# A gated linear scan feeding a mixture of experts on one core: ScalarE's list in the second group, and the path of y and x through DRAM in groups three and four

## The chip, the core and the metric

The kernel runs on one core of one Trainium2 chip. The metric is the device time of one execution in microseconds (us). Engines are called TensorE (PE in the views: matmuls; PEld: its weight loads), VectorE (DVE), ScalarE (ACT), GpSimd (POOL) and SyncE (SP, which here does little but issue DMAs, in the order of its list).

## The reference, cut to what matters

```
# attention: B=4 batches, H=8 heads, S=768 steps, D=48; complex state S (D x D) per head
a = a * min(|a|, 0.999) / (|a| + 1e-6)          # complex gate, one per step and row d
for t in range(S):
    S = a[t][:, None] * S + k[t][:, None] * v[t][None, :]
    y[t] = q[t] @ S.real
x = y as [3072 tokens, 384]                      # heads side by side
# mixture of experts: E=4 experts, F=1024
p = probs / (probs.sum(-1) + 1e-9)
out = sum over e of p[:, e] * (relu(x @ w1[e]) @ w2[e])
```

## The kernel before, in words

The 3072 tokens are cut into 12 groups of 256 (three to a batch), numbered 0 to 11, and a group into two chunks of 128. The work falls into a first part, up to about 600 us of the profile, and a second.

In the first part the experts 0 and 1 are applied to one group after another by `moe1`. A group has eight pairs, numbered 0 to 7, of two 128-wide slices of F: `w1_step` makes `ph` (18 matmuls, L179), ScalarE makes `hh` (L188) and VectorE `hl` (L189) out of it, and `w2_step` (12 matmuls, L198) adds them into `po`, one pair later. Each product is made three times, of high and low parts: weights `whi`, `wlo`, activations `xha`, `xla`, and `hh`, `hl`. `ph3_2` is group 3's pair 2; `po` carries the number of the pair with which its expert began, so that `po3_0` gathers pairs 0 to 3.

While group g goes through `moe1`, the attention of group g+1 is made and the preparation of later groups goes on. For each group that is:

- `norm`: the gate is scaled. ScalarE and VectorE take turns on tiles `s`, `u` and `A`: squares (L322, L323), a sum (L324), Ln (L333), Exp (L334), Square (L342), a product (L343), Identity (L344), then L346, L348, L349 and the scaling of `A` (L351).
- `prefix`: cumulative products of `A` on VectorE (L359 to L362, L302 to L310).
- `finish` and `front`: ScalarE L421, L422, L427 and L428, VectorE L425, then `Q` (L430) and `K` (L445 to L449). From the third group on both go to DRAM and back (`q_d`, `k_d`, L459 and L466) into `Qst` and `Kst`, of which there is one each. Groups 0 and 1 turn K on TensorE instead (`ktp`, `kp`, with ScalarE evicting into `KT` and `Kst`).
- `attention`: `ktp` (K turned), `dp` (the state's increment, L518), `sc` (scores, L530), `yp` (values, L546 and L551), evicted into `y` by ScalarE (L558). Groups 0 to 2 turn y into x on TensorE (`xp`, L582). Later groups store y to DRAM (`store_y`, L623) and read it back as `xa` (`load_x`, L159); `split_x` makes `xha` (ScalarE, L166) and `xla` (VectorE, L168) of it, which the next group's `ph` reads.

`between(k)` is called ahead of pair k. At pairs `FIRST[g]`, +1 and +2 it takes the next piece of group g's attention; otherwise it advances the preparation by a budget of microseconds (`STEP`, `MORE`). A scheduler then decides the order of each engine's list by its own simulated times. `behind(a, b)` adds a dependency that only orders a after b on one engine, and so steers that scheduler. An engine works through its list in order, so that an instruction which waits holds up all that stand after it.

In the second part (`w1_full`, `w2_full`) experts 2 and 3 are applied to blocks of 512 tokens. The change touches nothing there.

Of the kernel before, what the change touches and what calls it, by code (L numbers as in the profile page):

```python
# [8 lines left out]
F32 = mybir.dt.float32  # L9
F32R = mybir.dt.float32r  # L10
AF = mybir.ActivationFunctionType
# [45 lines left out]
WARM = {6: "pq", 7: "tk"}  # L57
NSEL = 2
XSEL = 3
FIRST = {1: 5, 2: 5, 3: 4, 4: 4, 5: 3, 6: 3}  # L60
STEP = {1: 4.2, 2: 4.2, 3: 4.2, 4: 4.2, 5: 4.2}
MORE = (1.9, 1.9, 0.5)
HALF = (2, 3, 4, 5)
HOFF = 96
WIDE = 32 + P + 48
DMA_SCRATCH = 4096
# [2 lines left out]
def fast_path(ctx, tc, qkP, aP, vP, probsP, w, out, flag):  # L69
# [39 lines left out]
    def behind(ins, prev):  # L109
        tc.add_manual_dep(ins.ins, prev.ins.name,  # L110
                          mybir.DependencyInfo(mybir.DependencyClass.NoSync, mybir.DependencyReason.DATA),
                          reason="issue order")
# [41 lines left out]
        wts[i] = (hi, lo)  # L154
        return last_pe if ps is not None else None

    def load_x(g):
        x = moe.tile([P, NJ, G], F32, tag="x", name=f"xa{g}", bufs=1)
        nc.sync.dma_start(x, y_d[g].rearrange("(j p) t -> p j t", p=P))  # L159
        return [(slice(0, G), x)]  # L160

    def split_x(g, parts):
        xh = moe.tile([P, NJ, G], F32R, tag="xh", name=f"xha{g}")
# [65 lines left out]
    with ExitStack() as c1:  # L229
# [84 lines left out]
        def norm(g, A, parts=((0, SEG),), prev=(None, None)):  # L314
            s = tmp(f"s{g}")
            u = tmp(f"u{g}")
            for n, (lo, hi) in enumerate(parts):
                col = g if n == 0 else NG
                fs = slice(lo * MS, hi * MS)
                Af = A.rearrange("p c i m -> p c (i m)")[:, :, fs]  # L320
                m2, L, y0, v = s[:, 0, fs], s[:, 1, fs], u[:, 0, fs], u[:, 1, fs]
                ins = [nc.scalar.activation(m2, Af[:, 0], AF.Square)]  # L322
                sq = nc.scalar.activation(L, Af[:, 1], AF.Square)  # L323
                ins.append(nc.vector.tensor_tensor_reduce(m2, m2, L, scale=1.0, scalar=3e38,  # L324
                                                          op0=ALU.add, op1=ALU.min, accum_out=st_m2[:, col:col + 1]))
                for x, p in zip(ins + [sq], prev + prev[:1]):
                    if p is not None:
                        behind(x, p)
                if n > 0:
                    behind(ins[0], exp)  # L330
                    behind(sq, exp)
                yield 1.0
                ln = nc.scalar.activation(L, m2, AF.Ln, bias=m2b)  # L333
                exp = nc.scalar.activation(y0, L, AF.Exp, scale=-0.5, bias=lnb)  # L334
                if g == 1:
                    behind(ln, state["kt", 0, 1])
                    behind(exp, state["y", 0, 0])
                if g == 0 and n == 0:
                    nc.vector.tensor_tensor(v, m2, y0, op=ALU.mult)
                    nc.vector.scalar_tensor_tensor(v, v, 4.0 / CAP ** 2, y0, op0=ALU.mult, op1=ALU.mult)  # L340
                else:
                    nc.scalar.activation(v, y0, AF.Square, scale=2.0 / CAP)  # L342
                    nc.vector.tensor_tensor(v, m2, v, op=ALU.mult)  # L343
                last["lin"] = nc.scalar.activation(L, y0, AF.Identity, scale=2.0 * EPS / CAP, bias=neg1)  # L344
                yield 0.95
                nc.vector.scalar_tensor_tensor(y0, v, 3.0, y0, op0=ALU.subtract, op1=ALU.mult)  # L346
                yield 0.95
                nc.scalar.activation(v, v, AF.Square, bias=neg1, accum_out=st_w[:, col:col + 1])  # L348
                nc.vector.scalar_tensor_tensor(y0, y0, -1.0, L, op0=ALU.max, op1=ALU.mult)  # L349
                yield 0.95  # L350
                nc.vector.tensor_tensor(Af, Af, bc2(y0), op=ALU.mult)  # L351
                yield 1.75
# [264 lines left out]
            inc1()  # L617
            rotate(g)

        def store_y(g, y):  # L620
            yv = y_d[g].rearrange("(p u d) t -> u d p t", u=2, d=D)
            for u in range(2):
                nc.sync.dma_start(yv[u], y[u * IM:u * IM + D])  # L623

        def attention(g, QK):
            y = small.tile([M, HP, G], F32, tag="y", name=f"y{g}")
            (turn0, _, inc0, sc0, val0), (turn1, _, inc1, sc1, val1) = (chunk(g, c, QK[1], y) for c in range(CG))
            turn0()
            inc0()
            yield sc0()  # L630
            val0()
            t_factors(g)
            xs = [turn_x(g, 0, y)] if g < XSEL else None
            yield sc1()
            val1()
            if g < XSEL:
                xs.append(turn_x(g, 1, y))
            store_y(g, y)
            x = xs or load_x(g)
            turn1()  # L640
            inc1()
            rotate(g)
            yield x

        def moe1(g, xh, xl, between=None, prev=None):
            def done(e, po):
# [102 lines left out]
            pass  # L749
        for i in range(NPRE):  # L750
            split_w(i, wst[i] if i in wst else stage1(i, PRE), ((ps_o, "po"), (ps_h, "ph")), prev=lin,
                    prev_pe=state.get(WARM.get(i)), prev_lo=state["y", 0, 0] if i in WARM else None)
        tick = big.tile([1, 1], F32, name="tick")
        nc.gpsimd.tensor_copy(tick, Qst[0:1, 0, 1, 0:1])
        for i in range(NPRE, NF1):
# [334 lines left out]
```

## Time and profile before

| | us |
|---|---|
| median of three runs (1009.35 to 1009.71) | 1009.37 |
| the profiled execution, its own time | 1010.7 |
| its span, from first to last instruction | 1008.9 |
| TensorE busy | 980.6 |
| VectorE busy | 589.9 |
| ScalarE busy | 363.5 |

The profile is of one execution, whose span leaves 1.8 us around it. Busy time of TensorE is the sum of its matmuls' pipelined spans; time that it is not busy is split by what it waited for. The granted clock is the share of full speed at which TensorE was let run: 0.997 over the span, and 1.00 in every stretch shown below.

### The profile page before, as it was taken

What the parts mean: (1) busy time and instruction counts of PE and PEld (TensorE: products, weight loads), DVE (VectorE), ACT (ScalarE), POOL (GpSimd) and SP (SyncE); (2) the same over time, 40 slices, a digit from 0 to 9 for tenths busy, and PEclk for the clock granted to TensorE, in tenths of its full rate; (3) what the DMA queues carried; (4) which work ended last, traced back from release to release, by engine and by line L of the source; (5) the groups of instructions that cost most, each with busy time, mean ns of one, the idle gap of its engine ahead of it and who ended that gap; (6) DMA issues with size and microseconds to landing.
All of it is one profiled execution on the core that took longest, in us unless ns stands there. A gap on an engine that the chain in (4) does not pass through costs nothing.

```text
span 1008.9 us, 16256 instructions
## 1 busy us (share of the span) xinstructions
PE 980.6 (97%) x6618; PEld 919.3 (91%) x6618; DVE 589.9 (58%) x1228; ACT 363.5 (36%) x652; POOL 35.7 (4%) x66
## 2 busy tenths in 40 slices
PE   5899999999999999999999999999999999999997
PEld 2799999999999999999999999999999899989996
DVE  7789989898988989698942463232132322321221
ACT  7755536446364453636422352121111211211110
POOL 6030000000000000000000000000000000000000
PEclk9999999999999999999999999999999999999999
DMA  9584277383674736547171780020030110100001
GB/s 305 174 170 135 63 189 156 120 220 95 166 192 122 213 109 160 154 122 204 64 166 39 252 305 32 1 94 32 1 126 1 37 58 1 63 1 1 32 1 35
DMA packets 88676, 111.15 MB, mean 110 GB/s; under 512 B 5840, under 2 KB 72960, under 8 KB 88592
## 3 DMA queue, kind: packets, MB, share of 16 engines
q1 hardware_dynamic: 84016, 94.11, 33.4%
q0 software_dynamic: 4576, 15.91, 5.3%
q8 instruction: 54, 0.88, 0.4%
q14 instruction: 30, 0.25, 0.1%
HBM read 74.09 MB, written 35.90 MB: 109 GB/s over the span
## 4 chain that ended last, share of the span: by engine, by line
PE 89%; ACT 4%; DMA 3%; DVE 2%; issue 1%; DVEq 0%; SPq 0%; ACTq 0%
PE pob L862 20%; PE phb L849 20%; PE ph L179 18%; PE po L198 18%; PE sc L530 4%; PE dp L518 3%; PE yp L551 2%; PE yp L546 2%; PE ktp L500 1%; DMA y_d<-y 1%; PE xp L582 1%; DMA wst<-w 1%; DMA xa<-y_d 1%; DMA q_d<-Q 0%; ACT whi L138 0%
## 5 line engine op out<-in xcount | busy, mean ns | idle before, releaser
L855 DVE SCALAR_TENSOR_TENSOR hlb<-phb,hhb 128x512 fp32r<-128x512 f32 x96 | 66.4, 691 | 270.6 <-ACT hhb L854 270.6
L854 ACT ACTIVATE hhb<-phb 128x512 fp32r<-128x512 f32 x96 | 57.3, 597 | 314.5 <-PE phb L849 299.1
L198 PE MATMUL po<-whi,hh 128*128 128x384 f32 x384 | 129.5, 339 | 0.5 <-ACT hh L188 0.4
L862 PE MATMUL pob<-wlo,hhb 128*128 128x384 f32 x384 | 129.2, 337 | 0.0
L862 PE MATMUL pob<-whi,hhb 128*128 128x384 f32 x384 | 128.9, 336 | 0.0
L198 PE MATMUL po<-wlo,hh 128*128 128x384 f32 x384 | 128.8, 335 | 0.0
L198 PE MATMUL po<-whi,hl 128*128 128x384 f32 x384 | 123.7, 339 | 1.3 <-DVE hl L189 1.3
L862 PE MATMUL pob<-whi,hlb 128*128 128x384 f32 x384 | 120.4, 336 | 0.0
L188 ACT ACTIVATE hh<-ph 128x512 fp32r<-128x512 f32 x96 | 57.2, 596 | 151.4 <-PE ph L179 141.8
L179 PE MATMUL ph<-xha,whi 128*128 128x256 f32 x576 | 103.9, 287 | 0.6 <-ACT xha L166 0.6
L179 PE MATMUL ph<-xha,wlo 128*128 128x256 f32 x576 | 102.1, 284 | 0.0
L179 PE MATMUL ph<-xla,whi 128*128 128x256 f32 x576 | 101.0, 283 | 0.0
L189 DVE SCALAR_TENSOR_TENSOR hl<-ph,hh 128x512 fp32r<-128x512 f32 x96 | 66.0, 688 | 47.8 <-ACT hh L188 46.7
L849 PE MATMUL phb<-xhb,whi 128*128 128x512 f32 x288 | 91.8, 392 | 0.0
L179 PEld LDWEIGHTS ph<-xha,whi 128*128 128x128 f32 x576 | 85.8, 190 | 2.1 <-ACT xha L166 1.1
L179 PEld LDWEIGHTS ph<-xha,wlo 128*128 128x128 f32 x576 | 83.1, 190 | 0.0
L179 PEld LDWEIGHTS ph<-xla,whi 128*128 128x128 f32 x576 | 82.6, 191 | 0.4 <-DVE xla L168 0.2
L849 PE MATMUL phb<-xlb,whi 128*128 128x512 f32 x288 | 82.7, 392 | 0.0
L849 PE MATMUL phb<-xhb,wlo 128*128 128x512 f32 x288 | 82.3, 393 | 0.0
L862 PEld LDWEIGHTS pob<-whi,hhb 128*128 128x128 f32 x384 | 72.1, 188 | 3.7
L862 PEld LDWEIGHTS pob<-wlo,hhb 128*128 128x128 f32 x384 | 72.1, 188 | 3.3
L198 PEld LDWEIGHTS po<-whi,hh 128*128 128x128 f32 x384 | 72.4, 189 | 1.3 <-ACT acc L649 0.7
(165 smaller groups left out, 1563.7 us busy)
## 6 DMA issues: line engine op xcount, KB each, us to landing
wst<-w SPq DMA_DIRECT2D x24, 384.0 KB, 5.8
qk<-qkP SPq DMA_DIRECT2D x24, 384.0 KB, 7.2
acc_d<-acc POOLq DMA_DIRECT2D x24, 384.0 KB, 4.1
prev<-acc_d SPq DMA_DIRECT2D x24, 384.0 KB, 4.7
A<-aP SPq DMA_DIRECT2D x22, 384.0 KB, 8.3
q_d<-Q SPq DMA_DIRECT2D x12, 387.0 KB, 4.1
Qst<-q_d SPq DMA_DIRECT2D x12, 387.0 KB, 5.8
v<-vP SPq DMA_DIRECT2D x24, 192.0 KB, 2.5
```

The costliest lines, as they stand in the source:

```text
L179: ins = nc.tensor.matmul(ph[:, u, :], wt[:, j * P:(j + 1) * P], xt[:, j, :], start=(n == 0), stop=(n == 3 * NJ - 1))
L188: wts["hh"] = nc.scalar.activation(hh, ph, AF.Relu)
L189: nc.vector.scalar_tensor_tensor(hl, ph, 0.0, hh, op0=ALU.max, op1=ALU.subtract)
L198: nc.tensor.matmul(po[t], ht[:, u, t * P:(t + 1) * P], wt[:, HD:], start=(i % FE == 0 and n == 0), stop=(i % FE == FE - 1 and n == 2))
L518: nc.tensor.matmul(d_ps[:, h, :], KT[:, h, :], vc[:, h * D:(h + 1) * D], start=True, stop=True)
L530: ins = nc.tensor.matmul(s_ps[:, h, :], Kc[:, hf * 4 + h, :], Qc[:, hf * 4 + h, :], start=True, stop=True)
L546: ins = nc.tensor.matmul(yo, st[:, o:o + n], Qc[:, o // D, :], start=True, stop=False)
L551: ins = nc.tensor.matmul(yo, vc[:, o:o + n], sc[h // 4][:, h % 4, :], start=first, stop=True)
L849: nc.tensor.matmul(ph, wt[:, j * P:(j + 1) * P], xt[:, j, :], start=(n == 0), stop=(n == 3 * NJ - 1))
L854: nc.scalar.activation(hh, ph, AF.Relu)
L855: nc.vector.scalar_tensor_tensor(hl, ph, 0.0, hh, op0=ALU.max, op1=ALU.subtract)
L862: ins = nc.tensor.matmul(po[t], ht[:, t * P:(t + 1) * P], wt[:, HD:], start=(i % FE == 0 and n == 0), stop=(i % FE == FE - 1 and n == 2))
```

## The change

Four edits, and what the scheduler makes of them.

1. `norm(1)`, the second group's: its Exp was ordered behind the eviction of the first chunk's y of group 0 (`state["y", 0, 0]`), and is now ordered behind the eviction of group 0's second `Kst` (`state["kst", 0, 1]`).
2. The low parts of weights 6 and 7 (`wlo6`, `wlo7`, four copies on ScalarE) were ordered behind that same eviction of y, and are now ordered behind `norm(1)`'s Square.
3. In groups 3 and 4 (`XHALF`) the store of y, the load of x and the split into `xha` and `xla` are made chunk by chunk: four stores of 96 KB for two of 192 KB, two loads of 192 KB for one of 384 KB, two copies on ScalarE and two subtractions on VectorE of 128x384 for one each of 128x768. The first chunk's come ahead of the second chunk's scores.
4. `FIRST[4]` goes from 4 to 3: the pieces of group 4's attention are taken at pairs 3, 4 and 5 of group 3's experts.

```
 XSEL = 3
-FIRST = {1: 5, 2: 5, 3: 4, 4: 4, 5: 3, 6: 3}
+FIRST = {1: 5, 2: 5, 3: 4, 4: 3, 5: 3, 6: 3}
...
+XHALF = (3, 4)
...
-    def load_x(g):
-        x = moe.tile([P, NJ, G], F32, tag="x", name=f"xa{g}", bufs=1)
-        nc.sync.dma_start(x, y_d[g].rearrange("(j p) t -> p j t", p=P))
-        return [(slice(0, G), x)]
+    def load_x(g, ts=slice(0, G), x=None):
+        if x is None:
+            x = moe.tile([P, NJ, G], F32, tag="x", name=f"xa{g}", bufs=1)
+        nc.sync.dma_start(x[:, :, ts], y_d[g].rearrange("(j p) t -> p j t", p=P)[:, :, ts])
+        return [(ts, x[:, :, ts])], x
...
                 if g == 1:
                     behind(ln, state["kt", 0, 1])
-                    behind(exp, state["y", 0, 0])
+                    behind(exp, state["kst", 0, 1])
...
-                    nc.scalar.activation(v, y0, AF.Square, scale=2.0 / CAP)
+                    last["sq"] = nc.scalar.activation(v, y0, AF.Square, scale=2.0 / CAP)
...
-        def store_y(g, y):
+        def store_y(g, y, ts=slice(0, G)):
             yv = y_d[g].rearrange("(p u d) t -> u d p t", u=2, d=D)
             for u in range(2):
-                nc.sync.dma_start(yv[u], y[u * IM:u * IM + D])
+                nc.sync.dma_start(yv[u][:, :, ts], y[u * IM:u * IM + D, :, ts])
...
-            xs = [turn_x(g, 0, y)] if g < XSEL else None
+            xs, x = [turn_x(g, 0, y)] if g < XSEL else [], None
+            if g in XHALF:
+                store_y(g, y, slice(0, C))
+                xs, x = load_x(g, slice(0, C))
             yield sc1()
             val1()
             if g < XSEL:
                 xs.append(turn_x(g, 1, y))
-            store_y(g, y)
-            x = xs or load_x(g)
+            rest = slice(C, G) if g in XHALF else slice(0, G)
+            store_y(g, y, rest)
+            if g >= XSEL:
+                xs = xs + load_x(g, rest, x)[0]
...
-                    prev_pe=state.get(WARM.get(i)), prev_lo=state["y", 0, 0] if i in WARM else None)
+                    prev_pe=state.get(WARM.get(i)), prev_lo=last["sq"] if i in WARM else None)
```

**ScalarE at the end of the start-up** (about 41 to 49 us of the profile before). Here `kp_1` is the second chunk's turned K of group 0, `yp` its values, `u_489` and `s_488` the tiles of group 1's `norm`, `lp` the low parts of weights 6 and 7, and `xp` group 0's turned y. Before:

```order
L510 ACTIVATE Kst<-kp_1_4_426 112x4x128
L558 ACTIVATE y_298<-yp_0_432 112x4x128
L334 ACTIVATE u_489<-s_488,lnb 128x768
L151 ACTIVATE wlo_569<-lp_0_571 128x384
L151 ACTIVATE wlo_569<-lp_1_575 128x384
L151 ACTIVATE wlo_580<-lp_0_582 128x384
L151 ACTIVATE wlo_580<-lp_1_586 128x384
L342 ACTIVATE u_489<-u_489 128x768
L344 ACTIVATE s_488<-u_489,neg_83 128x768
L166 ACTIVATE xha_608<-xp_0_456 128x3x128
L558 ACTIVATE y_298<-yp_1_463 112x4x128
L348 ACTIVATE u_489,st_w<-u_489,neg_83 128x768
```

And now (line numbers are two higher from `norm` on):

```order
L512 ACTIVATE Kst<-kp_1_4_426 112x4x128
L336 ACTIVATE u_489<-s_488,lnb 128x768
L560 ACTIVATE y_298<-yp_0_432 112x4x128
L344 ACTIVATE u_489<-u_489 128x768
L346 ACTIVATE s_488<-u_489,neg_83 128x768
L152 ACTIVATE wlo_569<-lp_0_571 128x384
L152 ACTIVATE wlo_569<-lp_1_575 128x384
L152 ACTIVATE wlo_580<-lp_0_582 128x384
L152 ACTIVATE wlo_580<-lp_1_586 128x384
L168 ACTIVATE xha_608<-xp_0_456 128x3x128
L350 ACTIVATE u_489,st_w<-u_489,neg_83 128x768
L560 ACTIVATE y_298<-yp_1_463 112x4x128
```

The Exp moved ahead of the first eviction of y, Square and Identity ahead of the four `wlo` copies, and the last of the norm's steps (L348, now L350) ahead of the second eviction of y. Further on, group 1's first L421 and L422 (now L423 and L424) moved ahead of the eviction of group 0's first expert (`acc0_0`, L649), behind which they stood.

**Group 4's preparation and attention.** ScalarE, where group 3's x is split (`xha3`), with group 4's `finish` (`s24`, `u24`, `Q4`) and the last pair of group 2 (`hh2_7`). Before:

```order
L188 ACTIVATE hh2_6_2351<-ph2_6_2332 128x512
L166 ACTIVATE xha3_2367<-xa3_2283 128x768
L421 ACTIVATE s24_1972<-A4_1505 128x768
L422 ACTIVATE s24_1972<-A4_1505 128x768
L188 ACTIVATE hh2_7_2412<-ph2_7_2393 128x512
L427 ACTIVATE u24_1973<-s24_1972,a2b_91 128x24x16
```

And now:

```order
L190 ACTIVATE hh2_6_2354<-ph2_6_2335 128x512
L168 ACTIVATE xha3_2370<-xa3_2204 128x3x128 x2
L423 ACTIVATE s24_1972<-A4_1505 128x768
L424 ACTIVATE s24_1972<-A4_1505 128x768
L429 ACTIVATE u24_1973<-s24_1972,a2b_91 128x24x16
L438 ACTIVATE Q4_1974<-A4_1505 128x12
L324 ACTIVATE s5_2385<-A5_1969 128x768
L325 ACTIVATE s5_2385<-A5_1969 128x768
L429 ACTIVATE u24_1973<-s24_1972,a2b_91 128x24x16
L190 ACTIVATE hh2_7_2417<-ph2_7_2398 128x512
```

`hh2_7` went from behind the second square to behind the second L427 (now L429). On VectorE `hl2_7` went likewise from ahead of `Q4` (L430, two products) to behind it, behind a product of group 3's state (L572) and behind L324 of group 5's `norm`. TensorE, where group 4's scores stand among group 3's experts, before:

```order
L198 MATMUL po3_0_1_2486<-wlo6_569,hh3_3_2629 128x384
L518 MATMUL dp4_0_2660<-v4_0_2646,KT_164 112x48 x8
L530 MATMUL sc4_0_0_2671<-Qst_162,Kst_163 128x128 x4
L530 MATMUL sc4_0_1_2678<-Qst_162,Kst_163 128x128 x4
L198 MATMUL po3_0_0_2485<-whi6_568,hl3_3_2630 128x384
```

And now:

```order
L200 MATMUL po3_0_0_2490<-whi4_546,hh3_2_2581 128x384
L520 MATMUL dp4_0_2612<-v4_0_2598,KT_164 112x48 x8
L532 MATMUL sc4_0_0_2623<-Qst_162,Kst_163 128x128 x4
L532 MATMUL sc4_0_1_2630<-Qst_162,Kst_163 128x128 x4
L200 MATMUL po3_0_0_2490<-wlo4_547,hh3_2_2581 128x384
```

They stood in the products of pair 3 (weights 6 and 7) and stand in those of pair 2 (weights 4 and 5). Just ahead of this, TensorE's sixteen products of `yp3_1`, which had products of `ph` and `ktp` among them, now stand together.

**SyncE's list at group 6**, which no edit names, with y of group 6 (`y_d_105`, `xa`) and the Q and K of group 7. Before:

```order
L623 DMA y_d_105<-y_3664 48x4x256 x2
L159 DMA xa_3844<-y_d_105 128x3x256
L459 DMA q_d_3779<-Q_3456 128x3x258 x2
L491 DMA v_1_4123<-vP 128x384
L466 DMA Qst<-q_d_3779 48x8x258 x2
```

And now:

```order
L625 DMA y_d_105<-y_3674 48x4x256
L461 DMA q_d_3789<-Q_3466 128x3x258 x2
L625 DMA y_d_105<-y_3674 48x4x256
L468 DMA Qst<-q_d_3789 48x8x258 x2
L161 DMA xa_3854<-y_d_105 128x3x256
```

The load of group 6's x went from ahead of group 7's Q to behind its way to DRAM and back. ScalarE's list moved with it: L421, L422, L427 and L436 of group 7 now stand ahead of the eviction of group 6's second y.

## Rows read from the trace of the kernel before

**Rows 1.** Stretches: length, then busy time of PE, PEld, DVE, ACT, POOL; clock.

```profile
47.00:433.00 386.00, 379.37 (x3067) 366.40 (x3064) 337.32 (x757) 192.53 (x353) 15.26 (x23) 1.00 0.59 150
...
433.00:1001.00 568.00, 568.00 (x3342) 527.76 (x3341) 215.93 (x369) 135.52 (x232) 4.86 (x9) 1.00 0.23 71
```

**Rows 2.** Waits of TensorE: us in total, times, the longest.

```profile
PE xp L582 <- ACT y L558: 2.1, 3, 0.7
...
PE po L198 <- DVE hl L189: 1.3, 2, 0.9
...
PE sc L530 <- ACT Kst L510: 0.8, 1, 0.8
PE sc L530 <- issue: 0.7, 1, 0.7
```

**Rows 3.** Timeline of ScalarE, 42 to 45 us: start, duration, what, [idle before].

```profile
42.65 0.60 ACT L558 ACTIVATE y<-yp 112x512 f32<-112x512 f32 x1 [0.39 <-PE yp L551]
43.14 0.93 ACT L334 ACTIVATE u<-s,lnb 128x768 f32<-128x768 f32 x1
43.97 1.62 ACT L151 ACTIVATE wlo<-lp 128x384 fp32r<-128x384 f32 x4
```

**Rows 4.** Timeline of VectorE, group 1's first L425.

```profile
72.44 0.56 DVE L425 CUSTOM_DVE_ANT_1 s<-s 128x384 f32<-128x384 f32 x1 [1.41 <-ACT s L422]
```

**Rows 5.** The chain that ended last, 184 to 256 us: start, duration, what.

```profile
184.75 0.68 PE ph L179 x4
...
199.63 2.36 PE po L198 x12
...
204.14 2.48 PE po L198 x12
...
208.76 2.08 PE po L198 x12
...
220.13 1.85 PE sc L530 x16
...
252.91 2.50 PE po L198 x12
```

**Rows 6.** Timelines of SyncE and ScalarE, group 3's y and x.

```profile
188.10 0.94 SPq L623 DMA_DIRECT2D y_d<-y  x2
...
195.58 0.85 ACT L166 ACTIVATE xha<-xa 128x768 fp32r<-128x768 f32 x1 [5.35 <-DMA xa<-y_d]
```

**Rows 7.** Timelines of VectorE and SyncE, group 4's preparation.

```profile
199.57 0.69 DVE L189 SCALAR_TENSOR_TENSOR hl<-ph,hh 128x512 fp32r<-128x512 f32 x1
...
200.63 1.82 DVE L430 TENSOR_TENSOR Q<-A,qk 128x768 f32<-128x768 f32 x2
...
212.15 1.06 SPq L466 DMA_DIRECT2D Kst<-k_d  x2
```

**Rows 8.** DMA issues of 150 to 350 us: size, median us to landing.

```profile
k_d<-K SPq DMA_DIRECT2D x12, 192.0 KB, 2.6
Kst<-k_d SPq DMA_DIRECT2D x12, 192.0 KB, 5.0
...
k_d<-K SPq DMA_DIRECT2D x4, 384.0 KB, 3.2
```

**Rows 9.** Timelines of ScalarE and TensorE at group 4's x.

```profile
242.63 0.84 ACT L166 ACTIVATE xha<-xa 128x768 fp32r<-128x768 f32 x1 [3.69 <-DMA xa<-y_d]
...
247.10 0.44 PE L198 MATMUL po<-whi,hh 128*128 128x384 f32 x1 [0.36 <-ACT hh L188]
...
250.48 0.52 PE L179 MATMUL ph<-xha,whi 128*128 128x256 f32 x3
```

**Rows 10.** Timelines of VectorE, SyncE and TensorE at group 6's x.

```profile
324.99 0.56 DVE L425 CUSTOM_DVE_ANT_1 s<-s 128x384 f32<-128x384 f32 x1 [2.88 <-ACT s L422]
...
330.45 3.58 SPq L466 DMA_DIRECT2D Qst<-q_d  x2
...
336.26 0.52 PE L179 MATMUL ph<-xha,whi 128*128 128x256 f32 x3
```

More of the change, by code (lines that the diff above doesn't have):

```diff
@@ L642, in attention @@
             rotate(g)
-            yield x
+            yield xs
         def moe1(g, xh, xl, between=None, prev=None):
```

## The prediction

> **What bounds the kernel now.** I read the stretches first. Between 433 and 1001 us TensorE is busy for every one of 568 us, so that no change of order can make that stretch shorter [rows 1]. Between 47 and 433 us, where the whole change lies, it is busy for 379.4 of 386 us: 6.6 us idle, at a granted clock of 1.00, the higher of its two levels [rows 1]. The edits hardly add or remove work for TensorE, so they can win only what it waits. The waits say where that is: three turns of x on ScalarE's y (2.1 in all), two times on hl (1.3), once on Kst out of ScalarE (0.8), once on a late Kst from DRAM (0.7, shown as "issue"), and small ones [rows 2]. The chain shows a second kind of loss that counts as busy: a block of twelve po that takes 2.08 undisturbed takes 2.36 at 199.6, 2.48 at 204.1 and 2.50 at 252.9, since its products start as hl comes out [rows 5]. Those excesses are 0.28, 0.40 and 0.42. VectorE is busy for 337.3 of the 386 us, 87% [rows 1]: close enough to full that a place lost in its list is felt in TensorE. The reader should take from this that the stake is 6.6 + 1.1 = 7.7 us at the very most, and that each part of it hangs on one instruction of ScalarE, VectorE or SyncE being in time.
>
> **Part A: Exp, Square and the wlo copies (edits 1 and 2).** No instruction is added or removed. Before, the first eviction of y waited 0.39 for TensorE until 42.65, so ScalarE was free at 42.26, and the Exp began at 43.14 [rows 3]. Now it begins at 42.26. The Square stood behind the four copies, so at 43.97 + 1.62 = 45.6 [rows 3]; now it stands behind Exp (0.93) and y (0.60), at 43.8: 1.8 sooner, and the products of VectorE that follow likewise. What hides the copies in their new place: weights 6 and 7 are not read before pair 3 of group 0, three blocks of twelve po (2.08 each [rows 5]) and as many of ph later. What pays: the eviction of the second y now has L348 ahead of it, and TensorE waits for that eviction already (one of the three xp waits, 0.7 [rows 2]); by ScalarE's times that adds 0 to 0.1, and I take 0.1.
>
> The lead goes on to group 1's first K on VectorE. One place could eat it: at 72.44 VectorE waited 1.41 for L422 [rows 4], which stood behind the eviction of an expert's result. In the new list it stands ahead of that eviction, so the lead passes. Then the wait of group 1's scores for Kst, 0.8 [rows 2], finds Kst there. It is worth 0.8, at most 1.0 with the slow start of its matmuls, and nothing if the lead is lost on the way. I take 0.9 less the 0.1: **-0.8**, bounds -1.0 and +0.1.
>
> **Part B: y and x by chunk, and group 4's attention a pair sooner (edits 3 and 4).** First, when group 3's x arrives. Before, 7.5 us passed from the first store of y, 188.10, to the copy of the landed x, 195.58 [rows 6]. The four ph matmuls (0.68) that stood among yp3_1 in the chain [rows 5] now stand behind it, so y is evicted 0.7 sooner. The last store and load are half as large. No row shows y or x at that size; the nearest is k_d, a store to DRAM like y's: 3.2 us at 384 KB, 2.6 at 192 KB [rows 8], 0.6 for half the bytes. Twice that is 1.2, so the second half of x is at ScalarE at 195.6 - 0.7 - 1.2 = 193.7. The bounds are 194.9, if a half takes as long as the whole, and 191.6, if all that lies behind the issuing of the stores (7.5 - 0.9) is halved. I take 193.7, since the row it rests on is a transfer of the same kind.
>
> The Trainium skill, in "DMA: Bandwidth & Descriptors", section "Anatomy of one DMA", gives one transfer about 2.0 us that do not depend on its size plus its bytes at 436 GB/s, fitted on another issuing path. By that page the two halves would save an estimated 0.2 and 0.4 us, x would be there half a microsecond later than I take it, and the whole sum would come to an estimated 1009.1. The k_d rows agree that the fixed part is the larger, and make the part that shrinks larger than the page does.
>
> The earlier x does not reach TensorE, for the new order has spent it. On VectorE hl2_7 began at 199.57 [rows 7], and the po block that reads it was 0.28 too long [rows 5]: there is no slack. Now hl2_7 stands behind Q4 (1.82 [rows 7]), a product of the state (about 0.5) and L324 (0.9, a pass over a tile of the size of one of Q4's two). Before, Q4 ended at 200.63 + 1.82 = 202.45, 6.9 behind the start of x's copy, with hl2_7's 0.6 inside and the copy of x whole. Without the one and with half of the other (0.4 less), it ends 5.9 behind. Then 0.5, 0.9 and hl2_7's 0.7 follow: hl2_7 ends 8.0 behind, at 201.7, where it ended at 200.26. TensorE stands 1.4 us more, 0 to 2.6 by the bounds. In exchange the 0.40 of the block at 204.14 goes, as hl3_0 is then no later than before and its reader is.
>
> Next, Kst. Group 4's scores stand one pair sooner, which is 4.2 us: twelve po, 2.08, and the gap up to the next block, 208.76 - 204.14 - 2.48 = 2.14 [rows 5]. They also stand behind one product of the block instead of four (0.5). They began at 220.1 [rows 5], and would want Kst at 215.4, or at 216.4 with the net 1.0 lost so far. Its transfer was issued at 212.15 [rows 7] and takes 5.0 to land [rows 8]: 217.1. In SyncE's list it still stands behind the stores of both chunks of K4, which hang on VectorE, where nothing is sooner; so the issue stays where it was. A wait of 0.7 appears, 0 to 1.7 by the bounds. All of pair 2's other products are queued behind it, so it is paid in full.
>
> Then group 4's own x. Before, ScalarE waited 3.69 for it until 242.63; hh3_7 and hl3_7 were late behind that copy, so that TensorE waited 0.36 at 247.10, the twelve po from there to 250.48 took 3.38 instead of 2.08, and the block at 252.9 had 0.42 too much [rows 5, 9]: 0.36 + 1.30 + 0.42 = 2.1. With the attention 4.2 us sooner and y in halves, x is there by 239 or so and none of this is left: -2.1, or half of it at the worst.
>
> Sum for B: +1.4 - 0.4 + 0.7 - 2.1 = **-0.4**, bounds -2.8 (no new wait, and the 0.28 and 0.40 gone) and +1.5. The added copy on ScalarE, subtraction on VectorE, and two stores and a load on SyncE lie where these engines wait for x anyway (5.35 us on ScalarE [rows 6]) and cost nothing. Were that cover gone, SyncE would pay 0.47 for each of three issues [rows 6], 1.4 us.
>
> **Part C: group 6.** No edit speaks of it, but SyncE's list does. The load of x6 now stands behind Qst7, whose issue ran from 330.45 to 334.0 as it waited for q_d7 [rows 10]. If Q7 came no sooner, x6 would be loaded from 334.0, land some 3.2 later (as k_d's 384 KB [rows 8]) and be copied (0.85 [rows 6]) by 338.1; ph6_0 wants it at 336.26 [rows 10]: 1.8 lost. But before, VectorE's L425 at 324.99 waited 2.88 for L422 [rows 10], which stood behind the eviction of y6; now it stands ahead. I give half of the 2.88 back and keep **+0.4**, bounds 0 and +2.1.
>
> Sum: -0.8 - 0.4 + 0.4 = -0.8. The profiled execution took 1010.7 for a span of 1008.9, and 1009.9 is what the sum makes of it. It stood 1.3 above the median of the runs shown, so the same difference is taken from the median: 1009.4 - 0.8 = **1008.6 us**. A measurement here can tell about 0.2%, 2.0 us, from no change.
>
> **The rivals.**
> - *The stall at group 4's x goes and nothing takes its place.* It decides if x3 lands before 192.3, so that hl2_7 ends by 200.3 in its new place, and K4 comes with it. Then B gives -2.8, A -0.9, and C nothing: 1005.7; with the late Kst of group 7 (0.7 [rows 2]) gone too, 1005.0. For it: 6.6 us of round trip lie open to be halved. Against it: the k_d rows give back 1.2 of them, not 2.6. Chance 0.26.
> - *The wait only moves.* Attention is taken a pair sooner, but the preparation that feeds it is not: 2.0 at hl2_7 and 1.2 at Kst stand against the 0.4 and 2.1 that go, B is +0.7, and the time 1009.4 - 0.8 + 0.7 + 0.4 = 1009.7. For it: hl2_7 and Kst both stood without slack. Against it: the x3 of the sum would have to come half a microsecond later. Chance 0.20.
> - *Slower: x6 queues behind q_d7.* If Q7 is not sooner, ph6_0 starts when the DMA chain lets it, at 338.1 instead of 336.26, whatever TensorE won in A and B, which it then waits off there: 1009.4 + 1.8 = 1011.2, and 1011.8 if ScalarE's list, with group 8's norm ahead of the copy, adds 0.6. It decides once Q7 is less than about 1 us sooner. For it: Q7 hangs on prefix work of a VectorE with little slack. Against it: the 2.88 us of idle time just ahead of Q7. Chance 0.16.
> - *The forecast itself:* some of the waits go and new ones take half of it back, 1006.8 to 1009.6. Chance 0.38.
>
> **How the numbers follow.** Faster by more than 0.2% (under 1007.35): nearly all of the first rival, 0.25, and a quarter or so of the forecast, 0.11: 0.36. Slower (over 1011.4): half of the third or a little more, 0.10, and 0.03 of the second: 0.13. The rest, 0.51, is within 0.2%. The range runs from 1005.2 to 1011.0; it leaves out 0.08 below and 0.12 above.
>
> **What would show it.** A right: Square at about 44 us, and no wait of sc on Kst near 89 us. B right: group 3's x copied in halves, the second near 193.7; a block of po near 200 us that takes over 3 us; a wait of sc near 216 us; no wait of TensorE between 246 and 254 us. C right: a wait of ph on xha near 336 us of under 1 us. The prediction is wrong if the lead of A also takes away waits on y at 101 or 151 us, which I count as staying, if hl2_7 isn't late, or if new waits stand in groups 7 to 9, where the scheduler has redrawn lists as well and I count nothing.

## The result and the profile after

The changed kernel is slower: its median is 1011.51 us where the kernel before had 1009.82 beside it, a ratio of 1.0016 (1.0010 to 1.0022), 1.7 us. Forecast were 0.8 us less, 1008.6, and at most 1011.0. Two later comparisons gave 1.0017 (1.0008 to 1.0026) and 1.0016 (1.0006 to 1.0026). In the first of these two the profiled execution ran at a granted clock of 0.82 and took 1812.8 us, so it is left out and has no row in the table below.

The execution profiled with the result took 1013.27, 1.8 above its median, and 1.0 of that lay ahead of the first ph matmul. The rows below are of another execution of the same kernel, whose span is 1008.9 like that of before and whose first ph starts within 0.04 us of before's. (Its time, 1010.65, is near the median of its own runs, 1010.59; the profiled execution of before stood 1.3 above its median. So equal spans don't mean equal kernels.) First the stretch that the change touches, with the columns of [rows 1]:

```profile
47.00:433.00 386.00, 377.82 (x3071) 367.24 (x3066) 337.11 (x758) 192.66 (x354) 15.31 (x23) 1.00 0.60 151
```

TensorE is idle for 8.2 us there, where it was 6.6. The waits of TensorE say on what; the view is that of [rows 2], and line numbers are two higher than before:

```profile
PE xp L584 <- ACT y L560: 2.1, 3, 0.7
PE ph L181 <- ACT xha L168: 1.7, 2, 1.1
PE po L200 <- DVE hl L191: 1.2, 1, 1.2
PE po L200 <- ACT hh L190: 1.1, 1, 1.1
...
PE sc L532 <- DVE A L364: 0.6, 1, 0.6
PE ph L181 <- DVE xla L170: 0.4, 1, 0.4
PE sc L532 <- DMA qk<-qkP: 0.3, 1, 0.3
```

The wait of sc on Kst out of ScalarE (0.8) is gone, and so are the stalls on hh and hl between 246 and 254 us. New are a wait on hh (1.1), a longer one on hl (1.2), one on group 6's x (1.1 of the 1.7) and one on xla (0.4). TensorE's timeline gives their places:

```profile
154.56 0.62 PE L181 MATMUL ph<-xla,whi 128*128 128x256 f32 x3 [0.41 <-DVE xla L170]
...
158.78 0.45 PE L200 MATMUL po<-whi,hh 128*128 128x384 f32 x1 [1.09 <-ACT hh L190]
...
202.21 0.62 PE L200 MATMUL po<-whi,hl 128*128 128x384 f32 x2 [1.25 <-DVE hl L191]
...
337.39 0.61 PE L181 MATMUL ph<-xha,whi 128*128 128x256 f32 x3 [1.14 <-ACT xha L168]
...
346.59 0.68 PE L532 MATMUL sc<-Qst,Kst 112*128 112x128 f32 x4 [0.34 <-DMA qk<-qkP]
```

The first two, together 1.5 us, stand at a place that the prediction doesn't mention. ScalarE's timeline shows why:

```profile
155.55 0.62 ACT L429 ACTIVATE u<-s,a2b 128x384 f32<-128x384 f32 x1 [0.63 <-DVE st_a L427]
156.07 0.21 ACT L438 ACTIVATE Q<-A 128x12 f32<-128x12 f32 x1
156.18 0.83 ACT L324 ACTIVATE s<-A 128x768 f32<-128x768 f32 x1
156.92 0.83 ACT L325 ACTIVATE s<-A 128x768 f32<-128x768 f32 x1
157.65 0.60 ACT L429 ACTIVATE u<-s,a2b 128x384 f32<-128x384 f32 x1
158.16 0.57 ACT L190 ACTIVATE hh<-ph 128x512 fp32r<-128x512 f32 x1
```

The hh of 158.16 is hh2_0, group 2's first. Before, it stood ahead of the first of the two Ln (L427, now L429):

```profile
156.57 0.58 ACT L188 ACTIVATE hh<-ph 128x512 fp32r<-128x512 f32 x1
157.30 0.62 ACT L427 ACTIVATE u<-s,a2b 128x384 f32<-128x384 f32 x1
```

Now it stands behind the second, as hh2_7 does in the rows of the order shown above, one group earlier. So the redrawn list repeats itself group by group, and I had looked at it in one.

Place A is as forecast. ScalarE:

```profile
42.11 0.94 ACT L336 ACTIVATE u<-s,lnb 128x768 f32<-128x768 f32 x1
42.94 0.60 ACT L560 ACTIVATE y<-yp 112x512 f32<-112x512 f32 x1
43.42 0.85 ACT L344 ACTIVATE u<-u 128x768 f32<-128x768 f32 x1
44.15 0.94 ACT L346 ACTIVATE s<-u,neg 128x768 f32<-128x768 f32 x1
44.98 1.63 ACT L152 ACTIVATE wlo<-lp 128x384 fp32r<-128x384 f32 x4
```

The Exp is at 42.1 instead of 43.1 and the Square at 43.4 instead of 45.5 or so [rows 3]. At group 3's x (SyncE, then ScalarE, then VectorE):

```profile
187.76 0.92 SPq L625 DMA_DIRECT2D y_d<-y  x2
191.54 0.38 SPq L161 DMA_DIRECT2D xa<-y_d  x1
...
194.11 0.53 ACT L168 ACTIVATE xha<-xa 128x384 fp32r<-128x384 f32 x1 [2.86 <-DMA xa<-y_d]
...
198.38 1.83 DVE L432 TENSOR_TENSOR Q<-A,qk 128x768 f32<-128x768 f32 x2
...
201.47 0.69 DVE L191 SCALAR_TENSOR_TENSOR hl<-ph,hh 128x512 fp32r<-128x512 f32 x1
```

From the first store of the last chunk to the copy it is 6.35 us, where it was 7.5 [rows 6]; and hl2_7 ends at 202.2, 8.0 behind that copy. Group 6's x on SyncE, with its landing, before:

```profile
325.23 0.38 SPq L159 DMA_DIRECT2D xa<-y_d  x1
327.57 1.19 SPq L459 DMA_DIRECT2D q_d<-Q  x2
...
340.99 1.41 SPq L466 DMA_DIRECT2D Kst<-k_d  x2
```

```profile
xa<-y_d SPq DMA_DIRECT2D x1, 384.0 KB, 3.2
```

And now:

```profile
323.72 1.26 SPq L461 DMA_DIRECT2D q_d<-Q  x2
325.07 1.08 SPq L625 DMA_DIRECT2D y_d<-y  x1
328.05 1.38 SPq L468 DMA_DIRECT2D Qst<-q_d  x2
329.53 0.41 SPq L161 DMA_DIRECT2D xa<-y_d  x1
...
335.07 1.23 SPq L461 DMA_DIRECT2D k_d<-K  x2
339.12 1.28 SPq L468 DMA_DIRECT2D Kst<-k_d  x2
```

```profile
Qst<-q_d SPq DMA_DIRECT2D x2, 387.0 KB, 5.7
...
xa<-y_d SPq DMA_DIRECT2D x1, 384.0 KB, 6.9
```

Q7 goes out at 323.72, where it was 327.57 before, and Qst7 is issued 2.4 us sooner than in [rows 10]. The load of x6 is issued at 329.5, far ahead of the 334.0 that the prediction took, but it lands 6.9 us after its issue, where it took 3.2 before. Two transfers of 387 KB, Qst7, were put on the queue just ahead of it; that these are the cause is shown below, where x6 and Qst7 change places and x6 lands in 3.8 (pin_c).

### The profile page after: what moved, and what is told of

The parts are those of the page before. It is cut to its first block, busy times and chain, and to the rows that moved or that the text cites. A ratio compares the mean times of both kernels' runs of the same rounds, so it can differ in the third digit from the quotient of the medians.

```text
span 1011.6 us, 16265 instructions
## 1 busy us (share of the span) xinstructions
PE 980.5 (97%) x6618; PEld 920.6 (91%) x6618; DVE 590.1 (58%) x1230; ACT 363.8 (36%) x654; POOL 35.6 (4%) x66
## 4 chain that ended last, share of the span: by engine, by line
PE 88%; DVE 3%; ACT 3%; DMA 3%; issue 1%; DVEq 0%; ACTq 0%; SPq 0%
PE pob L869 20%; PE phb L856 20%; PE po L200 18%; PE ph L181 18%; PE sc L532 4%; PE dp L520 3%; PE yp L553 2%; PE yp L548 2%; PE ktp L502 1%; DMA y_d<-y 1%; DMA Kst<-k_d 1%; DMA xa<-y_d 1%; PE xp L584 1%; PE qp L392 0%; DMA k_d<-K 0%
```

## The experiments

To see where each kernel gains and loses I read, from TensorE's timeline, when the first ph matmul of groups 0, 1, 3, 5 and 9 starts, and take the difference to the profile of the kernel before (51.47, 104.79, 197.32, 291.05, 475.43). The table gives by how much each stretch between them grew. "Scores up" says whether the list of TensorE has group 7's first scores ahead of ph6_2 (25 matmuls or about 3.5 us further up; in pin_d 13 matmuls or 1.5 us) or not: before they stood among ph6_2, and with `FIRST[7] = 3` they stand behind it.

| kernel | edits | scores up | group 0 starts | A: 0 to 1 | 1 to 3 | 3 to 5 | 5 to 9 | ratio to before |
|---|---|---|---|---|---|---|---|---|
| before, again | none | no | -0.05 | -0.03 | +0.03 | -0.33 | -2.22 | 1.0008 (0.9999 to 1.0018) |
| changed | 1, 2, 3, 4 | yes | +0.98 | -0.78 | +1.28 | -1.01 | +1.62 | 1.0016 (1.0010 to 1.0022) |
| changed, third run | 1, 2, 3, 4 | yes | -0.04 | -0.80 | +1.32 | -0.93 | -0.29 | 1.0016 (1.0006 to 1.0026) |
| norm_only | 1, 2 | no | 0.00 | -0.80 | +1.35 | -2.02 | -1.48 | 0.9990 (0.9981 to 0.9999) |
| no_norm | 3, 4 | no | -0.04 | -0.01 | -0.01 | -1.86 | -1.34 | 0.9998 (0.9989 to 1.0007) |
| no_half | 1, 2, 4 | yes | -0.01 | -0.78 | +1.29 | -1.56 | -0.39 | 0.9997 (0.9988 to 1.0006) |
| no_first | 1, 2, 3 | no | +0.19 | -0.78 | +1.30 | -1.57 | -1.58 | 0.9998 (0.9989 to 1.0007) |
| pin_c | all, Qst7 behind x6 | yes | +0.63 | -0.78 | +1.28 | -1.08 | +3.22 | 1.0039 (1.0026 to 1.0053) |
| pin_c_late7 | the same, FIRST[7] = 3 | no, later | +1.38 | -0.78 | +1.29 | -1.46 | -2.74 | 0.9990 (0.9981 to 0.9999) |
| pin_d | all, norm(4) behind hh2_0 | by 1.5 us | -0.08 | -0.78 | +0.82 | -3.36 | +1.67 | 0.9987 (0.9978 to 0.9996) |
| pin_d_late7 | the same, FIRST[7] = 3 | no, later | +0.08 | -0.78 | +0.81 | -3.40 | -3.02 | 0.9969 (0.9957 to 0.9981) |
| norm_pin | 1, 2, norm(4) behind hh2_0 | no | -0.03 | -0.80 | +0.82 | -2.18 | -1.76 | 0.9979 (0.9970 to 0.9988) |

The row "before, again" is the yardstick: the first profile of before held, in groups 5 to 9, 2.2 us that its second did not. Among them are the 0.7 on Kst7 [rows 2] and a wait of 0.4 at 431 us, both gone in the second. Waits on transfers of groups 7 and 8 come and go between executions by a microsecond or two. The columns up to group 3 are steady to 0.1 us between kernels whose lists agree there, that of groups 3 to 5 to 0.1 in the changed kernel and to 0.3 in the one before. The columns are of one execution each, which stood from 1.0 us below (before, again) to 2.7 above (pin_d) the median of its runs, and the stretch behind group 9's start differs by up to 1.5 us more; the ratio compares the medians of many. Not all runs were on the same chip. A difference of 0.1% in the last column is no more than before showed against itself (1.0008).

**Edits 1 and 2 alone** (norm_only).

```
-                    behind(exp, state["y", 0, 0])
+                    behind(exp, state["kst", 0, 1])
...
-                    nc.scalar.activation(v, y0, AF.Square, scale=2.0 / CAP)
+                    last["sq"] = nc.scalar.activation(v, y0, AF.Square, scale=2.0 / CAP)
...
-                    prev_pe=state.get(WARM.get(i)), prev_lo=state["y", 0, 0] if i in WARM else None)
+                    prev_pe=state.get(WARM.get(i)), prev_lo=last["sq"] if i in WARM else None)
```

> The kernel before with edits 1 and 2 alone. Theory 1 (the loss sits in places where the scheduler redrew lists that no edit names; the one at group 2, 154 to 160 us, comes from edits 1 and 2): no wait of sc on Kst near 89 us (-0.95), the wait of po on hh near 159 us stays (+1.9), no late x6; 0.8 to 1.5 us slower than before. Rival 2 (edits 1 and 2 slow the start-up itself): ph0_0 about 1 us later than before in the profile, 1.5 to 2.5 us slower. Rival 3 (the loss is the price of the added DMAs and halved copies): about 1 us faster than before.

Measured: 0.9990, 1 us faster than before, about what before differs from itself. The gain at 89 us (-0.80) and the loss at group 2 are there as theory 1 has it:

```profile
154.64 0.62 PE L179 MATMUL ph<-xla,whi 128*128 128x256 f32 x3 [0.41 <-DVE xla L168]
158.85 0.44 PE L198 MATMUL po<-whi,hh 128*128 128x384 f32 x1 [1.08 <-ACT hh L188]
```

So that loss, which the prediction lacks, comes from edits 1 and 2. But I had missed that these two edits also take away the stall at group 4's x (groups 3 to 5: -2.02), with x whole and the attention no sooner. ScalarE shows how:

```profile
243.33 0.85 ACT L166 ACTIVATE xha<-xa 128x768 fp32r<-128x768 f32 x1 [1.11 <-DMA xa<-y_d]
```

The copy of x4 starts 0.7 later than in [rows 9], but it has moved behind two squares and two Ln that had stood behind it, so ScalarE stands still for 1.1 us there and not for 3.7, and hh3_7 comes 1.9 sooner. The total came out on the other side than expected, and it is the total that rival 3 had forecast; the next run decides about that one. Rival 2 falls, as group 0 starts where it did.

**Edits 3 and 4 alone** (no_norm), the changed kernel with the diff just shown undone.

> The changed kernel without edits 1 and 2, so y and x by chunk and FIRST alone. Theory 1: no wait near 159 us, hl2_7 ahead of Q4 again, x6 ahead of q_d7 again, and the stall at 246 to 254 us gone: 1.5 to 3 us faster than before, 3 to 4.5 faster than the changed kernel. Rival 2: the start-up is that of before, 1 us sooner than in the changed kernel, and no more than 1 to 1.5 us faster than that one. Rival 3: as slow as the changed kernel or slower, with the losses at the chunked transfers of groups 3 and 4.

Measured: 0.9998, no difference from before, and 0.2% faster than the changed kernel; less than theory 1 said on both counts. In its profile nothing is lost at group 2, x6 is ahead of q_d7, and groups 3 to 5 are 1.86 shorter, 1.5 more than the second profile of before. Beside that second profile the whole is only 0.7 us ahead at group 9, so part of what I expected against the first profile was that execution's own waits. The chunked transfers show no loss in the profile, and with edits 3 and 4 alone the time is not longer, against rival 3.

**Qst7 behind x6** (pin_c). One added order in the changed kernel; in the lists of all engines two rows of SyncE change places, nothing else.

```
-        nc.sync.dma_start(x[:, :, ts], y_d[g].rearrange("(j p) t -> p j t", p=P)[:, :, ts])
+        wts["xa"] = nc.sync.dma_start(x[:, :, ts], y_d[g].rearrange("(j p) t -> p j t", p=P)[:, :, ts])
...
-                qb()
+                qb(wts["xa"] if g == 7 else None)
```

> The changed kernel with one added order: Qst of group 7 is loaded behind x of group 6, so that x6 no longer waits for the way of Q7 to DRAM and back; nothing else moves. Theory 1: the wait of ph on xha at 337 us (1.6) goes, Qst7 lands 0 to 1 us later and may cost some of it at group 7's scores: 0.8 to 1.6 us faster than the changed kernel. Rivals 2 and 3: no difference beyond 0.3 us.

Measured: 1.0039, slower still. Against the 1.0016 of the changed kernel that is 0.2%, with intervals that at most touch. The wait on x6 is gone, as theory 1 said, and what it said of the time is wrong. The landings, then the waits of TensorE:

```profile
k_d<-K SPq DMA_DIRECT2D x2, 384.0 KB, 6.3
...
xa<-y_d SPq DMA_DIRECT2D x1, 384.0 KB, 3.8
```

```profile
PE sc L532 <- DMA Kst<-k_d: 3.6, 1, 3.6
```

The scores of group 7 waited 3.6 us at 349 us for Kst7. Its store, k_d7, was issued at the same 335 to 336 as in the changed kernel. So x6 was not what held group 6 and 7, or not alone: what is won at x6 is waited off at Kst7, and more. The rest is the price of the added order itself: with Qst7 issued later, k_d7 took 6.3 us to land, where it took 4.1 to 4.6 in the changed kernel and 2.7 before, and Kst7 was issued at 341.78, later than in either. That made the second form of theory 1: the fault lies in the scores of group 7, which stand further up TensorE's list in the changed kernel. For the changed kernel itself that is half of it: it loses 1.1 to 1.6 at x6 and only 0.2 to 0.3 at those scores.

**Group 4's squares behind hh2_0** (pin_d). One added order in the changed kernel: `norm(4)`'s first squares (L324, L325) stand behind hh2_0. The scheduler then also draws hl2_7 ahead of Q4, and x6 ahead of q_d7.

```
-                    for r in norm(g + 1, A[g + 1]):
+                    for r in norm(g + 1, A[g + 1], prev=(wts["hh"] if g == 3 else None, None)):
```

> The changed kernel with one added order: group 4's first squares (norm) stand behind hh2_0 on ScalarE, so hh2_0 comes 1.5 us sooner in the list; the scheduler then also puts hl2_7 ahead of Q4 and x6 ahead of q_d7. Theory 1: the waits at 159 us (most of 1.9), at 202 us (1.4) and at 337 us (1.6) go, the gains at 89 and 247 us stay: 3 to 4.5 us faster than the changed kernel, 1.5 to 3 faster than before. Rival 2: 1 us of start-up stays, at most 0.5 to 2 faster than before. Rival 3: within 0.5 us of the changed kernel.

Measured: 0.9987, some 2.9 us faster than the changed kernel's 1.0016 and 1.3 faster than before, just under what was expected. The waits at 159, 202 and 337 us are gone, and groups 3 to 5 gain 3.36. But in the execution profiled, the slowest of its eleven and 2.7 above their median, 2.1 of this lead is waited off at 346 us:

```profile
345.90 2.39 PE L532 MATMUL sc<-Qst,Kst 112*128 112x128 f32 x16 [2.11 <-DMA Kst<-k_d]
```

Here x6 is in time and Kst7 was issued 3.5 us sooner than before (337.50 for 340.99), and still it is late. The first form of theory 1 can't say that; the second does: group 6 is 3.4 sooner too, and the scores stand 1.5 us further up, which with the 0.7 waited before [rows 2] makes 2.2.

**The two kernels once more** (before_again, after_again).

> The kernel before once more, for a second profile of it on the chip of this call. If run to run spread explains the start-up and tail (theory 1): the sums of waits between 47 and 433 us repeat to 0.3 us (6.6), while the start-up (ph0_0 at 51.5) and the time behind the last matmul (7.1) move by up to 1 us each. If the waits themselves vary (rival 4), the ones on transfers, Kst7 at 349 us above all, move by over 0.5 us.

> The changed kernel once more on the chip of this call. Theory 1: 1.0 to 2.5 us slower than before; waits of 1.5 at 155 to 160 us, 1.4 at 202 us and 1.6 at 338 us repeat to 0.3 us, and ph0_0 is within 0.3 us of before's (so the 1 us of the first profile was chance). Rival 2 (edits 1 and 2 slow the start-up): ph0_0 again about 1 us later; norm_only, which has those edits, began at before's 51.5, which speaks against it. Rival 4: the wait at 338 us moves by over 0.5 us.

Measured: 1.0008 for before against itself, so that 0.1% is within chance; 1.0017 for the changed kernel, as expected. With before, TensorE's idle time between 47 and 433 us went from 6.6 to 5.5, so theory 1's 0.3 was wrong: rival 4 has a share, as the waits behind 340 us moved by over 0.5 us, and the start-up did not.

**Edits 1, 2 and 4** (no_half: `XHALF = ()`).

> The changed kernel without edit 3, so edits 1, 2 and 4. Its lists have hl2_7 ahead of Q4, but x6 still behind the way of Q7. Theory 1 in its new form (edits 1 and 2 alone win some 1 to 2 us net; what loses is x6 behind q_d7, which needs edits 1 and 2 together with 4): wait at 338 us of 1.5 to 2.5, 0.5 to 2 us slower than before and 2 to 3 slower than edits 1 and 2 alone. Rival 3 (the chunked transfers lose): as fast as edits 1 and 2 alone, about 1 us faster than before.

Measured: 0.9997, no slower than before, and 0.7 us (0.07%) slower than edits 1 and 2 alone, not 2 to 3. Theory 1 has the place right and the price too high; by the time alone this can't be told from rival 3, since the intervals of this kernel and of edits 1 and 2 alone overlap. x6 is late (1.07 at 336 us). Groups 5 to 9 cost 1.1 more than with edits 1 and 2, and groups 3 to 5 another 0.5. Edit 3 put on top of this makes the changed kernel: 0.2% slower, of which 0.6 us lie in groups 3 to 5, where hl2_7 moves behind Q4. Where the other 1.3 lie the profiles don't show: that of this kernel stood 0.9 above its median, so part of them may be its own waits on transfers.

**Edits 1 and 2 with hh2_0 ahead** (norm_pin: the diffs of norm_only and pin_d).

> Edits 1 and 2 alone with the added order that puts group 4's first squares behind hh2_0. Theory 1: against edits 1 and 2 alone the wait at 158 us (1.1) goes and those on xla (0.4) stay; x6 ahead of q_d7 as before: 2 to 3 us faster than before if the lead is not waited off at Kst of group 7, 0.5 to 1.5 us if it is (in the run with the same order on the changed kernel 2.1 of the lead were lost at 344 us).

Measured: 0.9979, 2.1 us faster than before and 1.1 than edits 1 and 2 alone. ScalarE now:

```profile
155.56 0.62 ACT L427 ACTIVATE u<-s,a2b 128x384 f32<-128x384 f32 x1 [0.64 <-DVE st_a L425]
...
156.69 0.58 ACT L188 ACTIVATE hh<-ph 128x512 fp32r<-128x512 f32 x1
157.16 0.83 ACT L322 ACTIVATE s<-A 128x768 f32<-128x768 f32 x1
```

hh2_0 starts 1.5 us sooner and the wait behind it is gone. Groups 1 to 3 get 0.5 shorter by it, from 1.35 to 0.82: the wait on xla stays, and part of the 1.1 must have been made good by group 3, at a place that no view here shows.

**Group 7's attention a pair later** (pin_d_late7, pin_c_late7: the two kernels with `FIRST[7] = 3`, which was 2 by default).

> The changed kernel with group 4's first squares behind hh2_0, and group 7's attention taken a pair later (FIRST[7] = 3). Theory 1, second form (the loss of groups 6 and 7 is the scores of group 7, which edits 1, 2 and 4 together move 3 to 4 us up TensorE's list, ahead of a Kst from DRAM that is no sooner): the wait of 2.1 at 344 us goes, 1 to 2.5 us faster than the same kernel without FIRST[7], about 2 to 3.5 us faster than before. Rival (the wait only moves to the next group: x7 or Kst8 late in its turn): within 0.7 us of the kernel without FIRST[7].

> The changed kernel with Qst of group 7 behind x of group 6 in SyncE's list (which alone was no gain, since 3.6 were then waited for Kst7) and FIRST[7] = 3. Theory 1, second form: neither the wait on x6 (1.6) nor that on Kst7 (3.6) is there; 2 to 3.5 us faster than with the order of Qst7 alone, 0 to 1.5 us faster than before, with the waits at 159 and 202 us left. Rival (the x6 wait was the loss and the added order has another flaw): as slow as the changed kernel.

Measured: 0.9969 and 0.9990, where the same kernels without it had 0.9987 and 1.0039: 1.8 and 4.9 us. In neither does TensorE wait for x6 or Kst7; the waits of the first, start-up left out, are these:

```profile
PE xp L584 <- ACT y L560: 2.1, 3, 0.7
...
PE kp L511 <- ACT KT L503: 0.6, 1, 0.6
PE ph L181 <- ACT xha L168: 0.6, 1, 0.6
PE ph L181 <- DVE xla L170: 0.4, 1, 0.4
```

k_d7 is issued at 334.32 and Kst7 at 336.93 there, 0.6 sooner than in pin_d (334.88 and 337.50), and that is now soon enough. The first time is as the second form of theory 1 said; the second is 1.0 faster than before, as said, but 4.9 better than pin_c where 2 to 3.5 was said. No wait moved to the next group. FIRST[7] = 3 also redraws the lists of groups 7 and 8: of the 6.0 us by which groups 5 to 9 of pin_c_late7 are shorter than those of pin_c, 3.9 lie between the first ph of group 6 and that of group 7, where the wait on Kst7 was, and 2.1 behind it. The place of the scores is not all of the gain. `FIRST[7] = 3` on the changed kernel alone, with x6 left behind Qst7, was not run.

**Edits 1, 2 and 3** (no_first: `FIRST[4]` back at 4).

> The changed kernel without edit 4, so edits 1, 2 and 3. x6 is ahead of q_d7 and group 7's scores stand where they stood. Theory 1, second form: waits at 159 us (1.1) and 202 us (1.4) stay, none on x6, at most 0.5 on Kst7; 0 to 1.5 us faster than before, and 1.5 to 3 faster than the changed kernel. Rival (hl2_7 behind Q4 is the main loss): within 1 us of the changed kernel.

Measured: 0.9998, 0.2% faster than the changed kernel, as expected. The waits at 159 (1.1) and 202 us (1.3) are there, none on x6, 0.2 on Kst7: hl2_7 alone doesn't make the loss.

**The changed kernel a third time** (after_third).

> The changed kernel once more, since the profile taken in its second run was disturbed. Theory 1, second form: the wait at 155 to 160 us (1.5), at 202 us (1.4) and what is waited for x6 and Kst7 together (1.6 to 2.5) repeat within 0.5 us; ph0_0 is within 0.3 us of before's 51.5, so that the 1 us of start-up in its first profile was chance. Rival 2 (its start-up is slower, as the three profiles of the changed kernel and the two with Qst7 held back share 0.6 to 1.4 us there): ph0_0 again 0.6 us late or more.

Measured: 1.0016, and a start-up as before's, so rival 2 falls. The waits repeat: 1.5, 1.25, and 1.14 + 0.34 for x6 and group 7's scores, where the first execution had 1.5, 1.25, and 1.60 + 0.23.

## Why the prediction was wrong

- **What bounds the kernel**: right. TensorE's waits between 47 and 433 us were the stake, and the kernels differ by what they wait there, start-up and transfers of chance left out.
- **Part A**, -0.8: right, -0.78 to -0.80 in every kernel with edits 1 and 2. L422's new place let the lead pass, and the wait at 89 us is gone.
- **Part B**, -0.4: its sum was near, and partly by luck. Groups 3 to 5 became 0.93 to 1.01 shorter, 0.6 to 0.7 of it beyond the second profile of before. By its steps: hl2_7 ends 8.0 us behind the copy and TensorE's wait is 1.25 to 1.4, where 1.4 was said; the stall at 246 to 254 us went whole, as said. But edits 1 and 2 take that stall away without edits 3 and 4 (norm_only, -2.02), and so do edits 3 and 4 without 1 and 2 (no_norm, -1.86): the -2.1 was there to be had once, and with all four edits groups 3 to 5 are longer than with either pair. The wait for Kst came, but not at 216 us: it is 0.3 to 0.6 long and stands at 222 us, ahead of a later block of scores. The view names other releasers, but in the two profiles of the changed kernel and in no_norm the last transfer of group 4's Kst lands 0.2 us ahead of that block. The 212.15 of [rows 7] is the first half of Kst only; the second was issued at 214.28 there and landed at 221.1, which the prediction didn't read. The halved transfers saved 7.5 - 6.35 = 1.1 us from first store to copy, where 1.2 was taken from the k_d rows. By the Trainium skill, "DMA: Bandwidth & Descriptors", section "Anatomy of one DMA", it would have been an estimated 0.7 (0.23 for 96 KB less and 0.45 for 192 KB less); the measurement is nearer to the rows.
- **The step that is missing.** The prediction counted no new wait ahead of 184 us but the 0.1 on y. One stands where I hadn't looked: hh2_0 and the second half of xla2 at 154 to 160 us, +1.3 us on groups 1 to 3. It comes from edits 1 and 2 (norm_only has it, no_norm hasn't), and one added order takes the wait on hh away (norm_pin, pin_d). Put beside the other terms as forecast, it turns -0.8 into +0.5.
- **The step that failed: part C**, +0.4. Its mechanism was named, that the lead of TensorE is waited off at a chain of DMAs whatever A and B win, but with two wrong terms. I let x6 land 3.2 us behind its issue, as when nothing is ahead of it, and gave back time for a sooner Q7. Q7 was sooner by more than I gave, and x6 was late all the same, as its landing took 6.7 to 6.9 behind Qst7's two transfers: TensorE waited 1.1 to 1.6 for it, where 0.4 was said. And I took x6 for the end of the chain. Behind it stands Kst7, which group 7's scores want some 3.5 us sooner in the new list, a move that I hadn't read in TensorE's order. Holding x6 harmless showed Kst7 and made it later (pin_c, 3.6 us); with both harmless the kernel is 2.6 us faster than the changed one (pin_c_late7, 0.9990 for 1.0016), part of it in groups 7 and 8. In groups 5 to 9 the changed kernel is 1.9 to 3.8 us longer than the second profile of before.
- **The sum, as measured**: third run of the changed kernel against the second of before, from the table: -0.77 for A, +1.29 for groups 1 to 3, -0.60 for groups 3 to 5, +1.93 for groups 5 to 9, in all +1.85, where the ratios of the medians, 1.0016 and 1.0017, make 1.6 to 1.7.
- **The chances.** They don't agree with the range: 0.12 was left out above 1011.0, and 0.13 was given to times over 1011.4. And B's upper bound of +1.5 is less than its own terms make at their worst, 2.6 - 0.4 + 1.7 - 2.1 = +1.8.
- **The rivals.** The third, slower, was the nearest: its time of 1011.2 to 1011.8 holds the measured one. That is luck in part: it put the whole loss at x6, which took 1.1 to 1.6, and the rest stands at group 2. Its condition was wrong: it was to decide once Q7 is less than 1 us sooner, and Q7 was 3 to 4 us sooner. A chance of 0.16 was too little, as I weighed x6 by the time of its issue alone.

That edits 1, 2 and 4 are needed together for the scores to move up is read from the lists: norm_only, no_norm and no_first have them where they were, and no_half has them up. Why the scheduler's own times put them there isn't explained by any run. With any of edits 1 and 2, 3, or 4 taken away the kernel is as fast as before (0.9998, 0.9997, 0.9998): the losses at groups 2, 4 and 6 outweigh the gains only where all four edits stand together.

## What to carry to other kernels

When a scheduler redraws the lists, edits at 43 us moved instructions at 158 us here, and together with others at 202 and 346 us: compare the whole lists, engine by engine, and list every place where an instruction that TensorE reads from has moved behind one that it doesn't, before pricing any. A gain ahead of a transfer is kept only if the transfer's own chain comes sooner too; take the next such gate behind each gain (here x6, then Kst7) and ask what it does. And a transfer's landing is read with what is on its queue just ahead of it, not from its median when alone (6.9 us for 3.2 here). Where two edits each take away the same stall, its price may be counted once only.

The best version found is the changed kernel with two more decisions, `norm(4)` behind hh2_0 and `FIRST[7] = 3` (pin_d_late7): 0.9969 of before, 3.1 us faster, and by the two ratios 0.9953 or so of the changed one.

## What was not expected of the hardware

The same 384 KB load of x landed 3.2 us after its issue when nothing was put on the queue shortly ahead of it (before), 6.7 to 6.9 when 774 KB had been, the first of them 1.5 us ahead (the changed kernel), and 3.8 when those 774 KB were issued just behind it instead (pin_c). The store k_d7 did likewise: 2.7 us before, 6.3 with Qst7's transfers issued 4.5 to 5 us ahead of it and still on their way (pin_c). Executions of one kernel, not all on the same chip, differed by 1.0 us in the start-up ahead of the first ph matmul, and by about 2 us between groups 5 and 9, in part by what is waited for transfers; ahead of 210 us the waits of TensorE on ScalarE and VectorE repeat in place, and in size to 0.2 us.
